# A fused agent attention and squared-ReLU layer: small products on TensorE get a timetable of chunks and one more place

## The chip, the cores and the metric

The kernel runs on one core of a Trainium2 chip. The metric is the time of one execution in microseconds of device time, as the median of several runs. A profiled execution was recorded beside them; its instructions are what the rows below show.

## What is computed

Per batch (B = 4, N = 12480 tokens of C = 128 channels, 49 agents) two softmaxes stand in a row, and their output feeds a two-layer network with squared ReLU (d_ff = 2048):

```python
def sm(a, b):
    s = scale * (a @ b.transpose(0, 2, 1))
    s = s - s.max(-1, keepdims=True)
    e = np.exp(s)
    return e / (e.sum(-1, keepdims=True) + 1e-09)
a2k = sm(agents, k)
agent_v = a2k @ v
q2a = sm(q, agents)
x = q2a @ agent_v                      # reshaped to 49920 x 128
h = np.maximum(x @ w_in, 0.0)
return h * h @ w_out
```

## The kernel before

The product `agent_v @ w_in` is folded into a table `aw` per batch (three parts: `hi` and `lo` of the agents' rows), so the first layer is a product of the softmax weights of a token (`w`, `x`) with `aw`. Tokens come in 52 blocks of 960, thirteen to a batch. A block is worked off in sixteen steps (`c` = 0..15 in the main loop, `k` over all blocks): two halves of 480 tokens, eight steps each, of which two make a pair.

**A pair on TensorE.** `first(k)` issues, for even `k`, four main first products (`h<-w,aw_hi`, 128 x 128 against 480 columns) and four row tiles (`h<-x,aw_ex`, 19 rows each, in four row groups). Then `second(k - 4)` issues twelve products into one bank `o`: four with `wo_half`, then eight with `wo_hi` and `wo_lo`. ScalarE makes `r` and `g_hi` of `h`, VectorE `gg`, a product in place of `h`, and `g_lo`; GpSimd the other `g_lo`. The order of all these on their engines is a chain, written by `queued`. The banks of `h` are three; a pair takes two, so the third `h` of a pair needs the bank that the pair before it freed with `gg`. At every eighth step `o` is done: VectorE reads it (`ob`, scaled by `down`), and `turn` flips, so that the next `o` and the small products (`psa`) exchange their two banks. The pair in which that happens has c = 4 or c = 12.

**Small products.** Beside the pairs, TensorE computes for later blocks: the scores of the queries (`queries`: eight products of 120 x 49 per block, `psa<-ag,qt`, in float32, two instructions each), four transposes of the softmax (`psa<-ident,e`), and for the next batch, in `background(b + 1)`: the scores of thirteen blocks of keys (`psa<-ag,kt`, eight products each), two products for the maxima, thirteen chunks of values (`psa<-vs,e`, eight products each), and seven products for the tables. A generator hands its products to `put`, which appends them to one list `fill`; `second` calls `share` ahead of its second, third and fourth product, so that a small product stands between two `wo_half`: places 1, 2, 3. At the first of these, `share` takes up to eight from `fill` (four where `many` is set, at c = 14 and 0) and deals them out in turn: eight as 3, 3, 2, four as 2, 1, 1; in the pair in which the bank changes, at places 2 and 3 only.

**When they come.** The generators are stepped by the main loop. `queries(g + 2)` loads `qt` at c = 2 and puts its scores at c = 14 of block g; in block g + 1 it goes on at c = 1 (`m`, `e` on VectorE), 2 (exp on ScalarE), 3 (`z`, the division on GpSimd), 8 (the transposes), 9 (`y`, `ph`, `half`), 10 (the DMAs of `w` and `x`). `background` is stepped when a credit, one per step, covers what it asked for (`yield 1`, `yield PACE`); a `yield 0` or `yield -1` asks for a spot for products: an even c, with c / 2 in `SPOTS`, or in `STILL` for the tables, and `fill` empty. While `fill` holds anything, `background` isn't stepped at all. A step may not be placed ahead of what `behind` and `marks` name; within that, each engine's order between the chain's links is the scheduler's choice.

## Time and profile before

| what | us |
|---|---|
| median of 3 runs | 1900.27 (1900.15 to 1901.13) |
| the profiled execution, its span | 1897.8 |
| outside the span, against the median | 2.5 |
| TensorE busy | 1874.5 |
| VectorE busy | 1645.2 |
| ScalarE busy | 1670.6 |
| GpSimd busy | 1334.8 |

The span is from the first to the last instruction. A line of the order of time below names the start in us from the span's start, the time from the start of the first to the end of the last of the merged instructions, the engine, the line of the code (L494 is the helper `queued`, so go by the tiles), the operation, what it writes and reads, and how many were merged; in brackets, the engine's idle time ahead of it and what ended that. The ends of matmuls are modelled and overlap the next start, so costs on TensorE are read from start to start.

### The profile page before, as it was taken

What the parts mean: (1) busy time and instruction counts of PE and PEld (TensorE: products, weight loads), DVE (VectorE), ACT (ScalarE), POOL (GpSimd) and SP (SyncE); (2) the same over time, 40 slices, a digit from 0 to 9 for tenths busy, and PEclk for the clock granted to TensorE, in tenths of its full rate; (3) what the DMA queues carried; (4) which work ended last, traced back from release to release, by engine and by line L of the source; (5) the groups of instructions that cost most, each with busy time, mean ns of one, the idle gap of its engine ahead of it and who ended that gap; (6) DMA issues with size and microseconds to landing.
All of it is one profiled execution on the core that took longest, in us unless ns stands there. A gap on an engine that the chain in (4) does not pass through costs nothing.

```text
span 1897.8 us, 31097 instructions
## 1 busy us (share of the span) xinstructions
PE 1874.5 (99%) x10848; PEld 1402.6 (74%) x10848; DVE 1645.2 (87%) x1918; ACT 1670.6 (88%) x1607; POOL 1334.8 (70%) x1270
## 2 busy tenths in 40 slices
PE   9799999999999999999999999999999999999999
PEld 9577777777678777777767877777767777777776
DVE  6877888888988888888998788888899989899887
ACT  4577999998887899999888789999888999999997
POOL 1555789896656589887666568889666676767675
PEclk9899999999999999999999999999999999999999
DMA  9233222221123222222112322222111111111110
GB/s 372 77 107 106 88 66 83 82 74 53 56 69 108 85 84 76 90 74 63 50 47 90 102 71 74 90 66 72 48 46 55 51 52 52 51 53 43 57 36 29
DMA packets 74148, 144.53 MB, mean 76 GB/s; under 512 B 9356, under 2 KB 45864, under 8 KB 73992
## 3 DMA queue, kind: packets, MB, share of 16 engines
q1 hardware_dynamic: 73992, 142.55, 23.6%
q8 instruction: 86, 1.41, 0.3%
q14 instruction: 70, 0.57, 0.1%
HBM read 82.89 MB, written 25.56 MB: 57 GB/s over the span
## 4 chain that ended last, share of the span: by engine, by line
PE 87%; DVE 7%; issue 2%; ACT 2%; POOL 1%; DMA 1%; SPq 0%; POOLq 0%; DVEq 0%; ACTq 0%
PE o L494 53%; PE h L494 24%; PE psa L494 10%; DVE gg L494 2%; ACT r L494 1%; DVE g_lo L494 1%; POOL g_lo L523 1%; ACT g_hi L494 1%; DVE h L494 1%; DMA raw<-in_w_in 1%; DVE aw_half L392 0%; DVE ob L494 0%; DMA ahead<-in_kT 0%; DVE rest L117 0%; DVE s L278 0%
## 5 line engine op out<-in xcount | busy, mean ns | idle before, releaser
L523 POOL TENSOR_TENSOR g_lo<-gg,g_hi 128x480 f16<-128x480 f32 x832 | 998.0, 1221 | 424.4 <-ACT g_hi L494 264.9
L494 ACT ACTIVATE r<-h 128x960 f32<-128x960 f32 x832 | 763.5, 967 | 113.7 <-PE h L494 56.4
L494 ACT ACTIVATE g_hi<-r 128x1920 fp32r<-128x1920 f32 x416 | 754.2, 1813 | 30.3 <-ACT r L494 0.7
L494 DVE TENSOR_TENSOR g_lo<-h,g_hi 128x960 f16<-128x960 f32 x416 | 479.9, 1154 | 126.2 <-ACT g_hi L494 93.8
L494 PE MATMUL o<-g_hi,wo_hi 128*128 128x480 f32 x1664 | 569.1, 423 | 0.0
L494 DVE TENSOR_TENSOR gg<-r,h 128x960 f32<-128x960 f32 x416 | 479.4, 1152 | 83.0 <-ACT r L494 78.7
L494 PE MATMUL o<-g_lo,wo_half 128*128 128x480 f16 x1664 | 516.9, 370 | 0.5 <-POOL g_lo L523 0.5
L494 PE MATMUL o<-g_hi,wo_lo 128*128 128x480 f32 x1664 | 496.1, 379 | 0.0
L494 DVE TENSOR_TENSOR h<-r,h 128x960 f32<-128x960 f32 x416 | 480.4, 1155 | 1.1
L494 PE MATMUL h<-w,aw_hi 128*128 128x480 f32 x1664 | 433.5, 381 | 6.9 <-DVE gg L494 4.1
L494 PEld LDWEIGHTS h<-w,aw_hi 128*128 128x128 f32 x1664 | 311.9, 189 | 62.7 <-DVE gg L494 10.7
L494 PEld LDWEIGHTS o<-g_hi,wo_hi 128*128 128x128 f32 x1664 | 314.7, 189 | 50.1 <-issue 0.8
L494 PEld LDWEIGHTS o<-g_hi,wo_lo 128*128 128x128 f32 x1664 | 312.6, 188 | 48.8
L494 PEld LDWEIGHTS <-wo_half 128*128 128x128 f16 x1664 | 171.9, 112 | 149.0 <-issue 96.7
L494 PE MATMUL h<-x,aw_ex 19*128 19x480 f16 x1664 | 159.1, 372 | 0.0
L494 PEld LDWEIGHTS <-aw_ex 19*128 19x128 f16 x1664 | 41.8, 91 | 138.3 <-issue 138.3
L494 PEld LDWEIGHTS psa<-ag,qt 128*120 128x120 f32 x816 | 127.6, 187 | 6.8 <-issue 0.3
L494 PE MATMUL psa<-ag,qt 128*120 128x49 f32 x816 | 118.3, 249 | 0.0
L428 POOL TENSOR_TENSOR e<-e,z 120x392 f32<-120x392 f32 x52 | 43.9, 845 | 74.3 <-DVE z L427 40.4
L286 POOL TENSOR_TENSOR vs<-vt,vs 120x1024 fp32r<-120x1024 f32 x39 | 85.8, 2201 | 0.0
L494 PEld LDWEIGHTS psa<-ag,kt 128*120 128x120 f32 x624 | 78.1, 184 | 5.1 <-DVE ob L494 2.5
L494 PE MATMUL psa<-ag,kt 128*120 128x49 f32 x624 | 76.7, 259 | 0.0
(147 smaller groups left out, 1086.3 us busy)
## 6 DMA issues: line engine op xcount, KB each, us to landing
qt<-in_qT SPq DMA_DIRECT2D x52, 480.0 KB
out_T<-ob SPq DMA_DIRECT2D x104, 240.0 KB
vt<-in_v SPq DMA_DIRECT2D x39, 516.0 KB
kt<-in_kT SPq DMA_DIRECT2D x39, 480.0 KB
w<-ph SPq DMA_DIRECT2D x102, 91.9 KB
w<-y SPq DMA_DIRECT2D x102, 91.9 KB
x<-half SPq DMA_DIRECT2D x416, 17.8 KB
ahead<-in_v SPq DMA_DIRECT2D x13, 516.0 KB
```

Source lines behind the costliest of these rows:

```text
L286: last[nc.gpsimd] = nc.gpsimd.tensor_sub(vs[:, :, C + 1 : 2 * C + 1], vt[:, :, :C], vs[:, :, :C].bitcast(F32))
L428: nc.gpsimd.tensor_mul(e, e, z.broadcast_to([TP, NT, NA]))
L494: ins = issue(*args, **kw)
L523: chain[nc.gpsimd] = nc.gpsimd.tensor_sub(lo[:, n, :], gg[:, n, :], hi[:, 0, n, :].bitcast(F32)).ins
```

## The change

`put` takes sizes and cuts a set of products into chunks; `fill` holds chunks, and one is taken per pair (`take`, before `first`). Its products are dealt out over places 1, 2, 3 as before, over 2 and 3 where the bank changes; a chunk of scores that goes on with a set, or has no chunk in the pair before it, uses places 1, 2, 3, 0. Place 0 is new: between the four main first products and the four row tiles, in `first`. Three plans replace the fixed numbers: "old" for blocks 0 and 1 of a batch with another to come (scores of queries put at c = 14, in 4 + 4), "dense" for blocks 2 and 3 (put at c = 12, in 3 + 5; the softmax one to two steps earlier; keys at c = 0 and 8 in 4 + 4, at c = 4 in one), "lean" for all others (put at c = 12, in 2 + 4 + 2). The sizes and the step of the put come from the plan of the next block (`then`). The maxima, values and tables ask for the same spots now ("lean": 1, 2, 3, 5), and `background` is held back only by chunks of its own, except where it wants a spot.

```diff
@@ -35,9 +35,18 @@
 PAIRED = (0, 2, 4, 6, 1, 3, 5, 7)
 OPEN = 10
 HELD = 1
-SPOTS = (1, 2, 3, 5, 6)
-STILL = (1, 3, 5)
 PACE = 1.4
+ONE = (NT,)
+TWO = (NT // 2, NT // 2)
+
+PLANS = {
+    "old": dict(put=14, sizes=TWO, early=(), late=(1, 2, 3, 8, 9, 10), spots=(1, 2, 3, 5, 6),
+                keys={p: ONE for p in (1, 2, 3, 5, 6)}),
+    "lean": dict(put=12, sizes=(2, 4, 2), early=(), late=(1, 2, 3, 8, 9, 10), spots=(1, 2, 3, 5),
+                 keys={p: ONE for p in (1, 2, 3, 5)}),
+    "dense": dict(put=12, sizes=(3, 5), early=(15,), late=(0, 1, 6, 7, 8), spots=(0, 1, 2, 4, 5),
+                  keys={0: TWO, 2: ONE, 4: TWO}),
+}
 
 
 @with_exitstack
@@ -184,13 +193,19 @@
 
 
     fill = []
-
-    def put(calls):
+    owner = [None]
+
+    def put(calls, sizes=None):
         if alone[0]:
             for call in calls:
                 call()
-        else:
-            fill.extend(calls)
+            return
+        assert not fill
+        at = 0
+        for n in sizes or (len(calls),):
+            fill.append((calls[at : at + n], sizes is not None, at > 0, owner[0]))
+            at += n
+        assert at == len(calls)
 
     def product(*args, **kw):
         def issue():
@@ -226,12 +241,12 @@
 
     def scores(b, i, kt):
         st = state.setdefault(b, {"s": []})
-        yield 0
+        sizes = yield -2
         ps = bank()
         sv = ps[:TP, : NT * NA].rearrange("p (t a) -> p t a", a=NA)
         put([
             product(sv[:, t, :], kt[:, t * TP : (t + 1) * TP], ag[:, b, :], start=True, stop=True) for t in range(NT)
-        ])
+        ], sizes)
         yield 1
         s = sp.tile([TP, NT, NA], F32, name="s")
         nc.scalar.copy(s, sv)
@@ -401,7 +416,7 @@
 
     weights = {}
 
-    def queries(g, early=None):
+    def queries(g, early=None, sizes=None):
         b = g // NB
         qt = qp.tile([C, BLK], F32, name="qt", bufs=1)
         nc.sync.dma_start(qt, qT[:, g * BLK : (g + 1) * BLK])
@@ -412,7 +427,7 @@
         put([
             product(sv[:, slots[t], :], qt[:, t * TP : (t + 1) * TP], ag[:, b, :], start=True, stop=True)
             for t in range(NT)
-        ])
+        ], sizes)
         yield
         m = qp.tile([TP, NT, 1], F32, name="m", bufs=1)
         nc.vector.reduce_max(m, sv, axis=AX.X)
@@ -507,6 +522,8 @@
             cs = slice((2 * c + n) * P, (2 * c + n + 1) * P)
             queued(nc.tensor.matmul, nc.tensor, out, state[b]["hi"][:, cs], w, start=True, stop=False)
 
+        for call in due[0]:
+            call()
         with tc.high_priority():
             for t, out in enumerate(outs):
                 rows = slice(t * 32, t * 32 + NL)
@@ -529,23 +546,32 @@
         queued(nc.vector.tensor_sub, nc.vector, lo, hs[1][:, :, :G], hi[:, 1].bitcast(F32))
         parts[k + 1] = hi[:, 1], lo
 
-    due = []
-
-    def share(n, new):
-        if n == 1:
-            calls = [fill.pop(0) for _ in range(min(len(fill), NT // 2 if many[0] else NT))]
-            due[:] = [[], [], [], []]
-            for at in range(len(calls)):
-                due[2 + at % 2 if new else 1 + at % 3].append(None)
-            for d in due:
-                for at in range(len(d)):
-                    d[at] = calls.pop(0)
-        for call in due[n]:
-            call()
+    due = [[], [], [], []]
+    busy = [False]
+
+    def take(swap):
+        for d in due:
+            d.clear()
+        before, busy[0] = busy[0], bool(fill)
+        if not fill:
+            return
+        calls, scored, on, _ = fill.pop(0)
+        if swap:
+            places = (2, 3)
+        elif scored and (on or not before):
+            places = (1, 2, 3, 0)
+        else:
+            places = (1, 2, 3)
+        counts = [len(range(n, len(calls), len(places))) for n in range(len(places))]
+        at = 0
+        for n, place in sorted(zip(counts, places), key=lambda x: x[1]):
+            due[place].extend(calls[at : at + n])
+            at += n
 
     def flush():
         while fill:
-            fill.pop(0)()
+            for call in fill.pop(0)[0]:
+                call()
 
     def second(k):
         g, i = divmod(k, SLOTS)
@@ -559,7 +585,8 @@
             todo += [(w[:, 2 * c + n, :], hi[:, n, :]) for w in (wo_hi, wo_lo) for n in range(2)]
         for n, (w, y) in enumerate(todo):
             if 0 < n < 4:
-                share(n, i % NP == 0)
+                for call in due[n]:
+                    call()
             queued(
                 nc.tensor.matmul, nc.tensor, o[:, :G], w, y,
                 start=(i % NP == 0 and n == 0), stop=(c == NP - 1 and n == len(todo) - 1),
@@ -595,12 +622,20 @@
 
     marks = []
 
-    def step(gen):
+    def waits(gen):
+        return any(of is gen for *_, of in fill)
+
+    def step(gen, sent=None):
+        assert not waits(gen)
+        owner[0] = gen
 
         with ExitStack() as es:
             for ins in behind + sum(marks[-2:-1], []):
                 es.enter_context(tc.issue_after(ins))
-            return next(gen, "end")
+            try:
+                return gen.send(sent)
+            except StopIteration:
+                return "end"
 
     def run(gen):
         for _ in gen:
@@ -679,8 +714,14 @@
 
     alone[0] = False
     ffn = ctx.enter_context(tc.tile_pool(name="ffn", bufs=4))
-    many = [False]
     later = None
+
+    def plan(g):
+        b, i = divmod(g, NB)
+        if b + 1 < B and i < 2:
+            return PLANS["old"]
+        return PLANS["dense" if i < 4 and b + 1 < B else "lean"]
+
     for k in range(total + LAG):
         if k < total:
             g, c = divmod(k, SLOTS)
@@ -694,11 +735,17 @@
             if i == 0 and c == 0 and b + 1 == B:
                 want = "end"
             credit = min(credit + 1.0, 5.0)
+            now, then = plan(g), plan(g + 1)
             for _ in range(2):
-                if want == "end" or (want <= 0 and (c % 2 or c // 2 not in (STILL if want else SPOTS))) or credit < want or fill:
+                if want == "end" or credit < want or waits(todo):
                     break
+                sent = None
+                if want <= 0:
+                    if fill or c % 2 or c >= then["put"] or c // 2 not in now["keys" if want == -2 else "spots"]:
+                        break
+                    sent = now["keys"][c // 2] if want == -2 else None
                 credit = credit - want if want > 0 else 0.0
-                want = step(todo)
+                want = step(todo, sent)
                 if k == 0:
                     credit = -6.0
                 if want is None:
@@ -707,14 +754,15 @@
             if g + 1 < B * NB:
                 if c == 0 and g:
                     ahead = later
-                if c in ((2, 3, 4, 5, 8, 9, 10) if g == 0 else (1, 2, 3, 8, 9, 10)):
+                if c in ((2, 3, 4, 5, 8, 9, 10) if g == 0 else now["late"]):
                     step(ahead)
             if g + 2 < B * NB:
                 if c == 2:
-                    later = queries(g + 2)
-                if c in (2, 14):
+                    later = queries(g + 2, sizes=then["sizes"])
+                if c in (2, then["put"], *then["early"]):
                     step(later)
-            many[0] = c in (14, 0)
+            if k % 2 == 0 and k >= LAG:
+                take((k - LAG) % NP == 0)
             if k % 2 == 0:
                 begun = first(k)
                 next(begun)
```

## Rows read from the trace of the kernel before

**Rows 1.** Page, part 1: busy us (share of the span) xinstructions

```profile
PE 1874.5 (99%) x10848; PEld 1402.6 (74%) x10848; DVE 1645.2 (87%) x1918; ACT 1670.6 (88%) x1607; POOL 1334.8 (70%) x1270
```

**Rows 2.** Waits of TensorE, whole span: us in total, times, longest

```profile
PE h L494 <- DVE gg L494: 4.1, 10, 0.8
...
PE psa L494 <- DVE ob L494: 1.6, 3, 0.7
```

**Rows 3.** Order of time, TensorE: plain pair, stalled pair, pair behind a late `gg`

```profile
1409.58 1.03 PE L494 MATMUL h<-w,aw_hi 128*128 128x480 f32 x4
...
1413.41 0.60 PE L494 MATMUL h<-w,aw_hi 128*128 128x480 f32 x2
1414.77 0.69 PE L494 MATMUL h<-w,aw_hi 128*128 128x480 f32 x2 [0.77 <-DVE gg L494]
...
1639.50 1.18 PE L494 MATMUL h<-w,aw_hi 128*128 128x480 f32 x4
```

**Rows 4.** Order of time, TensorE: quiet block, pairs at c = 14 and 0

```profile
1529.59 1.03 PE L494 MATMUL h<-w,aw_hi 128*128 128x480 f32 x4
...
1530.86 0.38 PE L494 MATMUL o<-g_lo,wo_half 128*128 128x480 f16 x1
...
1531.43 0.37 PE L494 MATMUL o<-g_lo,wo_half 128*128 128x480 f16 x1
1531.64 0.31 PE L494 MATMUL psa<-ag,qt 128*120 128x49 f32 x2
1531.79 0.37 PE L494 MATMUL o<-g_lo,wo_half 128*128 128x480 f16 x1
...
1534.07 1.03 PE L494 MATMUL h<-w,aw_hi 128*128 128x480 f32 x4
...
1538.56 1.03 PE L494 MATMUL h<-w,aw_hi 128*128 128x480 f32 x4
```

**Rows 5.** Order of time, TensorE: two pairs with keys, c = 2 and 4

```profile
121.29 1.03 PE L494 MATMUL h<-w,aw_hi 128*128 128x480 f32 x4
...
126.62 1.03 PE L494 MATMUL h<-w,aw_hi 128*128 128x480 f32 x4
...
132.13 0.38 PE L494 MATMUL h<-w,aw_hi 128*128 128x480 f32 x1
```

**Rows 6.** Order of time, weight loads of TensorE: the first pair of rows 4

```profile
1530.55 0.10 PEld L494 LDWEIGHTS <-aw_ex 19*128 19x128 f16 x4 [0.33 <-issue]
...
1530.86 0.61 PEld L494 LDWEIGHTS psa<-ag,qt 128*120 128x120 f32 x4
```

**Rows 7.** Groups by line: busy us, mean ns of one, idle before

```profile
L494 PE MATMUL psa<-ag,qt 128*120 128x49 f32 x816 | 118.3, 249 | 0.0
L494 PE MATMUL psa<-ag,kt 128*120 128x49 f32 x624 | 76.7, 259 | 0.0
L392 DVE CAST aw_half<-aw_lo 49x512 f16<-49x512 f32 x16 | 14.3, 894 | 0.4 <-DMA aw_ex<-aw_half 0.2
L387 DVE SCALAR_TENSOR_TENSOR aw_lo<-psa,rl,aw_hi 49x512 fp32r<-49x512 f32 x12 | 8.7, 725 | 0.0
```

**Rows 8.** Order of time, VectorE: quiet block from c = 0; late `gg`

```profile
1536.60 1.16 DVE L494 TENSOR_TENSOR gg<-r,h 128x960 f32<-128x960 f32 x1 [0.66 <-ACT r L494]
1537.67 0.56 DVE L418 TENSOR_REDUCE m<-psa 120x8 f32<-120x392 f32 x1
...
1545.27 1.15 DVE L494 TENSOR_TENSOR gg<-r,h 128x960 f32<-128x960 f32 x1
...
1558.92 0.71 DVE L494 TENSOR_SCALAR ob<-o,down 128x480 f32<-128x480 f32 x1
...
1638.76 1.15 DVE L494 TENSOR_TENSOR gg<-r,h 128x960 f32<-128x960 f32 x1 [0.35 <-issue]
```

**Rows 9.** Order of time, VectorE: an eviction of the tables beside `gg`

```profile
462.95 0.15 DVE L359 TENSOR_TENSOR bound<-psa,rl 98x1 f32<-98x1 f32 x1
463.17 1.15 DVE L494 TENSOR_TENSOR gg<-r,h 128x960 f32<-128x960 f32 x1
```

## The prediction

> **What bounds the kernel now.** I read the page's engine line first, then TensorE's waits, then its order of time pair by pair. A pair is the work of one even step: four main first products (`h<-w`), four row tiles (`h<-x`), four `wo_half` products with the small products among them, eight further `o` products; sixteen steps c = 0..15 make a block. TensorE is busy for 1874.5 us, 99% of the span [rows 1], and it waits longest in total for VectorE's `gg`, 4.1 us [rows 2]. So the time is the sum of what TensorE is given, and the reader should look at what a pair costs with and without small products. A pair without any takes 1413.41 - 1409.58 = 3.83 us [rows 3]. One with four score products of a row set takes 4.48, at c = 14 and again at c = 0 (1529.59, 1534.07, 1538.56) [rows 4]: 0.66 more. One with eight of keys takes 5.33, and 5.51 where they stand at two places only [rows 5].
>
> **Two prices.** At c = 14 the four stand 2, 1, 1 behind the first three `wo_half`; in the first key pair the eight stand 3, 3, 2. With s for the first product at a place and a for each further one, 3s + a = 0.66 and 3s + 5a = 1.50, so a = 0.21 and s = 0.15. The order of time says the same: two products between two `wo_half` make 1530.86 to 1531.43 = 0.57 us, one makes 0.36 (1531.43 to 1531.79) [rows 4], none 0.21. A product alone has its first weight load behind the 480 columns before it; one behind another product does not. Each product that leaves a neighbour and gets a place of its own saves 0.06 us.
>
> On this the Trainium skill (TensorE: Matmul & The Clock Gate, Part 3, The mechanism) speaks against the change: a weight load overlaps with running products only where the row groups differ. A score product fills the same rows as the `wo_half` before it, so by that rule nothing would be hidden, place or no place, and s would equal a. The two prices above do not agree with it; the load row shows the loads of `psa` starting at 1530.86, with the `wo_half` product [rows 6].
>
> **Row sets.** 816 instructions, two to a product, are 51 sets of eight [rows 7]; the first is issued in one go before the pairs begin to overlap, and the planner places 50. Its credits and spots, followed step by step through the code, give for the old version the pairs that the trace shows, and for the new one the counts below. Now a set costs 2 x 0.66 = 1.32. Under "lean" (39 of the 50) it becomes 2 + 4 + 2 products at c = 12, 14, 0, all alone, seven behind `wo_half` and one at place 0: 7 x 0.15 + p, with p the price of place 0. Under "old" (5 sets) seven of ten groups become 1, 1, 1, 1 and three stay 2, 1, 1. Under "dense" (6 sets) the groups are 2, 1 and 1, 2, 1, 1: five alone, two behind another, one at place 0: as dear as now.
>
> **Place 0** does not occur in the old trace, so p has to be bounded. Now the loads of the row tiles start at 1530.55, 0.33 us after the weight loads before them ended [rows 6], and 0.96 after the first of four `h` (1529.59) [rows 4]; with 0.22 from one `h` to the next that is 0.30 after the fourth, some 0.09 more than its columns need. A product in between has its first load behind the fourth `h`, as behind a `wo_half`; its second load shows, and the row tiles then wait their 0.09 as they did. So p = 0.15 to 0.16, nearest to the row of a product alone; I take 0.16. Below: if the 0.09 covered part of the second load, 0.10 or somewhat less. Above: 0.25, if the pause came twice. Place 0 is used 61 times (52 of rows, 9 of keys).
>
> So a lean set costs 1.05 + 0.16 = 1.21, 0.12 less than now within rounding: 39 x 0.12 = 4.6 us. The seven "old" groups save 0.05 each: 0.4. Dense: 0.
>
> **Keys.** 39 chunks of eight [rows 7]. Now 24 stand 3, 3, 2 (1.50 each) and 15 at two places (1.65, between 1.59 and the 1.68 of rows 5): 60.8 us. Then 17 stand 3, 3, 2, 13 at two places, and 9 are cut into 2, 1, 1 (0.66) and 1, 1, 1, 1 (0.61): 25.5 + 21.5 + 11.4 = 58.4. Saved: 2.3.
>
> **Background moved.** The maxima of the keys cost a stall where a product sits in the pair that changes banks and waits for `ob` (1.6 us in three [rows 2]); in the first batch it leaves that pair: about 0.6 saved. Later in each batch the four products that make `aw` now stand at least four steps apart; with the new spots three of them fall on c = 2, 4, 6 of one block. Each brings VectorE 0.73 + 0.89 = 1.62 us [rows 7], and a plain pair leaves it about 0.4 (3.83 less three operations of 1.15 [rows 8]). The old spacing already costs a stall of 0.77 before an `h` [rows 3], about 2 us in all such places of a batch. Closer together, but in longer pairs, I put them at 2.5: 3 x 0.5 = 1.5 lost, between 0 and 3. Values keep their pairs but for one or two chunks per batch. The steps that a waiting fill used to hold back may now go at c = 15 and 0; they are of other engines, the fullest of which, ScalarE, is busy for 88% of the span [rows 1]: nothing. The DMA of `qt` stays at c = 2, those of `w` and `x` at c = 10 (c = 8 in six dense blocks), with SyncE's queue otherwise as it was: nothing.
>
> **What the earlier products wait for.** In the pair at c = 12 they use the bank that `ob` has just read. `ob` ends at 1558.92 + 0.71 = 1559.63 in a quiet block [rows 8], 1.52 after that pair's start; the first product there comes at 1.69, with its load 0.2 earlier. That is barely free; in blocks with values `ob` is earlier.
>
> **What is late next.** The pair at c = 0 shrinks from 4.48 to 4.13. Just behind it VectorE is full: `m`, `e`, `z` of the softmax, then `gg` of c = 4, which ends at 1545.27 + 1.15 = 1546.42, 12.35 after c = 0 began [rows 8]. The third `h` of the pair at c = 6 needs that buffer. It would now stand at 4.13 + 2 x 3.83 + 0.44 = 12.22, so it would wait 0.2 us, and the next load with it. What decides is where `m` goes. Now the last score product stands behind the third `wo_half` and ends 1.27 + 0.57 + 0.36 + 0.21 + 0.31 = 2.72 after the pair's start [rows 4], at 1536.8, after `gg` started (1536.60), and VectorE has idled 0.66 us before that `gg`; `m` comes behind it, at 1537.67 [rows 8]. In the new order the last one stands behind the second `wo_half` and ends 1.27 + 0.36 + 0.21 + 0.31 = 2.15 after the start, 1536.2 in these rows. `m` (0.56) then fits largely into the idle time, and the chain ends some 0.3 earlier. That a small eviction is put ahead of `gg` when its product ends early has an example: `bound` at 462.95, before `gg` at 463.17 [rows 9]. I count on it: nothing lost.
>
> **The sum.** -4.6 - 0.4 - 2.3 - 0.6 + 1.5 = -6.4 us. The profiled execution spans 1897.8 us and the median is 1900.27; the 2.5 around the span does not depend on the change. 1897.8 - 6.4 = 1891.4, or 1893.9 as a median: I forecast 1894.0. That is 0.33% faster; 0.2% (3.8 us) is about what can be told from no change.
>
> **Rivals.**
> (1) VectorE takes the gain back. If `m` stays behind `gg`, each quiet lean block (11 of them, where TensorE has no values) waits 0.19 and loses the cover of one load. A late `gg`, ending at 1639.91, 0.41 after its pair began [rows 3, 8], made four `h` take 1.18 in place of 1.03 [rows 3, 4]. That is 0.19 + 0.10 = 0.29, times 11. In the 18 lean blocks with values, which are longer, I count one lost cover each, 0.12, as a bound. Together 5.4 lost: 1899.4. For it: VectorE without a gap through these pairs. Against it: rows 9.
> (2) Place 0 is cheaper, 0.10: 61 x 0.06 = 3.7 more gained, 1890.3. For it: the 0.09 pause is there anyway. Against: no row shows a weight load in it.
> (3) Place 0 is dearer, 0.25: 61 x 0.09 = 5.5 lost, 1899.5.
> (4) Slower: the four loads of the row tiles, which now start together within 0.10 us [rows 6], come one after another behind a small product, 3 x 0.09 later: p = 0.43, 61 x 0.27 = 16.5 lost, 1910.4. It turns slower from p = 0.27 on. Against it: those loads already wait until the `h` before them is through.
> (5) Places do not matter. If a lone product cost what a neighbour does, only the terms of the background would stay: 1900.27 - 0.6 + 1.5 = 1901.2. The page's rule above would give this; the two prices speak against it.
>
> **How the numbers follow.** Forecast 0.57, (1) 0.20, (2) 0.09, (3) 0.06, (4) 0.05, (5) 0.03. The forecast's own range is 1891 to 1897 (tables 0 to 3, the rest from rounding); 0.06 of its 0.57 lies above 1896.5. Range: down to (2) with nothing lost on the tables, 1889.5; up to (1) or (3), 1899.6. Left out: (4), (5) and edges, under 0.2. Faster by over 0.2%: 0.51 + 0.09 = 0.60. Slower by over 0.2%: (4) and a bad case of (1) with (3), 0.07. Within: 0.33.
>
> **What the new profile would show.** Pairs at c = 12, 14, 0 of a quiet block at 4.13, 4.43, 4.13 us (now 3.83, 4.48, 4.48). From the fourth `h` over a product at place 0 to the row tiles 0.46 where it is 0.30 now: this gives p. `m` ahead of `gg` in the pair at c = 0, and no wait of `h` for `gg` at c = 4 and 6; if `m` stands behind, (1). The tables' blocks at 11 and 12 of a batch longer by about half a us in sum. The forecast is wrong if p is above 0.25, if the stalls for `gg` come once per block, or if VectorE's backlog under three `aw` products in a row grows past 3 us in all.

## The result and the profile after

| | median, us | profiled span, us |
|---|---|---|
| before | 1900.27 (1899.67 to 1901.13, 5 runs) | 1897.8 |
| after | 1910.78 (1910.06 to 1911.09, 5 runs) | 1909.3 |

The ratio is 1.0054, 95% interval 1.0042 to 1.0067. The changed kernel is about half a per cent slower, where I had forecast 0.33% faster with a range that ended at 1899.6.

The engine line of the page, to be held against [rows 1], says little: TensorE is as full as it was, for 6.2 us longer, and the other engines do the same work.

```profile
PE 1880.7 (99%) x10848; PEld 1412.7 (74%) x10848; DVE 1647.1 (86%) x1918; ACT 1670.2 (87%) x1607; POOL 1335.0 (70%) x1270
```

TensorE's waits after (us in total, times, longest), to be held against [rows 2]. The waits for `gg` sum to no more than before, though one of them is now 1.4 long. New are a wait for a DMA, 1.7 us, and waits of the tables' own products for a bank that VectorE's `aw_lo` reads, 1.2 us.

```profile
PE h L509 <- DVE gg L509: 3.8, 4, 1.4
...
PE psa L509 <- DMA kt<-in_kT: 1.7, 1, 1.7
PE psa L509 <- DVE aw_lo L402: 1.2, 3, 0.4
```

Since waits and busy time do not tell where 11.5 us of span come from, I measured every block from the start of its first `h` to that of the next block's, in both traces, and summed the differences over blocks that do the same kind of work (us against the kernel before, one profiled execution each; the three last columns belong to experiments told further down; 1.6 of the +4.9 under "gate" is a drop of the clock that other executions do not have in that block):

| blocks | number | after | gate | gate_no_max | before_no_max |
|---|---|---|---|---|---|
| block 0 | 1 | +7.0 | +1.6 | +1.5 | +0.2 |
| "old" | 5 | -2.8 | -1.7 | -3.2 | -0.6 |
| "dense" | 6 | -3.9 | -2.7 | -2.7 | -0.7 |
| fifth block of batches 0 to 2 | 3 | +2.7 | +4.9 | -0.6 | -0.6 |
| lean, with values | 13 | +1.7 | +1.7 | -1.4 | -0.2 |
| lean, quiet | 11 | +1.7 | +1.9 | -1.5 | -0.3 |
| lean, with tables | 11 | +4.1 | +4.1 | -1.6 | -2.8 |
| start, last two blocks | | +1.0 | 0.0 | -0.2 | +0.4 |
| sum | | +11.5 | +9.8 | -9.8 | -4.6 |

There are four places that lose: block 0, the fifth blocks, the tables, and a little in each of the 24 other lean blocks. Each can be read from the trace.

**The quiet block.** Order of time on TensorE, pairs at c = 14, 0, 2, 4 and 6 (columns as in [rows 4]):

```profile
1539.54 1.03 PE L509 MATMUL h<-w,aw_hi 128*128 128x480 f32 x4
1540.41 0.31 PE L509 MATMUL psa<-ag,qt 128*120 128x49 f32 x2
1540.65 0.38 PE L509 MATMUL h<-x,aw_ex 19*128 19x480 f16 x4
...
1543.96 1.03 PE L509 MATMUL h<-w,aw_hi 128*128 128x480 f32 x4
...
1548.12 1.04 PE L509 MATMUL h<-w,aw_hi 128*128 128x480 f32 x4
...
1551.95 1.15 PE L509 MATMUL h<-w,aw_hi 128*128 128x480 f32 x4
...
1555.90 1.16 PE L509 MATMUL h<-w,aw_hi 128*128 128x480 f32 x4
...
1559.86 0.38 PE L509 MATMUL h<-w,aw_hi 128*128 128x480 f32 x1
```

The pairs with products take 4.42 (c = 14) and 4.16 (c = 0), as forecast. But the plain pairs at c = 4 and 6 take 3.95 and 3.96 in place of 3.83, and their four `h` span 1.15 and 1.16 in place of 1.03. The weight loads of the pair at c = 4, and VectorE from c = 0 on, say why:

```profile
1551.74 0.40 PEld L509 LDWEIGHTS h<-w,aw_hi 128*128 128x128 f32 x2
1552.39 0.30 PEld L509 LDWEIGHTS h<-w,aw_hi 128*128 128x128 f32 x2 [0.25 <-DVE gg L509]
```

```profile
1546.49 1.15 DVE L509 TENSOR_TENSOR gg<-r,h 128x960 f32<-128x960 f32 x1 [0.45 <-ACT r L509]
1547.56 0.56 DVE L433 TENSOR_REDUCE m<-psa 120x8 f32<-120x392 f32 x1
...
1551.19 1.16 DVE L509 TENSOR_TENSOR gg<-r,h 128x960 f32<-128x960 f32 x1
...
1555.16 1.15 DVE L509 TENSOR_TENSOR gg<-r,h 128x960 f32<-128x960 f32 x1
```

`m` stands behind `gg` as before, VectorE idles 0.45 us ahead of that `gg`, and the chain behind it is as long as it was: the third `gg` ends 1555.16 + 1.15 - 1543.96 = 12.35 after the pair at c = 0 began, to the hundredth what [rows 8] gave. The `gg` of c = 2 ends at 1552.35, and the third weight load of the next pair goes at 1552.39. TensorE comes earlier by what the pair at c = 0 lost, and stands. The matmul rows show no idle time there; the load row does. Over the whole span the group of these loads (busy us, mean ns, idle ahead of it and its main releaser) has 13.6 us behind `gg`, the kernel before 10.7; in the eleven quiet blocks alone it is 5.9 against 1.2:

```profile
L509 PEld LDWEIGHTS h<-w,aw_hi 128*128 128x128 f32 x1664 | 310.8, 189 | 65.4 <-DVE gg L509 13.6
```

VectorE has no idle time between that first `gg` and the third. But the `gg` of c = 2 (1551.19) also starts only 0.10 after the first of the two `r` in the row below is done (1551.09), and that `r` stands behind an exponential for which ScalarE waited 0.54 us, until VectorE had made `e` (ScalarE):

```profile
1549.69 0.53 ACT L437 ACTIVATE e<-e 120x392 f32<-120x392 f32 x1 [0.54 <-DVE e L435]
1550.13 1.82 ACT L509 ACTIVATE r<-h 128x960 f32<-128x960 f32 x2
```

So `m` and `e` behind the scores delay that `gg` in two ways, in VectorE's own order and by way of ScalarE.

**Blocks with values** lose in the pair at c = 2. The first product with values waits for the bank that VectorE's `e` reads until 775.92 + 0.56 = 776.48 (order of time, VectorE and TensorE):

```profile
775.92 0.56 DVE L435 TENSOR_TENSOR e<-psa,m 120x392 f32<-120x392 f32 x1
```

```profile
776.21 0.38 PE L509 MATMUL o<-g_lo,wo_half 128*128 128x480 f16 x1
776.62 0.57 PE L509 MATMUL psa<-vs,e 120*98 120x258 f32 x3
```

0.41 us lie between these two starts; in the kernel before it is 0.17 (770.88 and 771.05). The pair takes 5.11, before 4.87.

**Block 0.** Windows of the profile (busy us and number of instructions of PE, PEld, DVE, ACT, POOL; granted clock; DMA share; GB/s), first before, then after:

```profile
86.00:90.00 4.00, 4.00 (x16) 2.16 (x16) 2.96 (x5) 1.70 (x3) 2.36 (x2) 0.57 0.32 66
90.00:94.00 4.00, 4.00 (x28) 3.15 (x26) 3.50 (x6) 3.94 (x4) 1.65 (x2) 1.00 1.00 382
```

```profile
86.00:90.00 4.00, 4.00 (x17) 2.65 (x17) 3.50 (x5) 1.83 (x2) 2.12 (x3) 0.50 0.17 32
90.00:94.00 4.00, 2.32 (x11) 1.70 (x10) 3.19 (x6) 3.80 (x4) 1.15 (x2) 0.50 0.97 359
94.00:99.40 5.40, 5.40 (x20) 4.73 (x20) 1.63 (x2) 0.74 (x2) 2.36 (x2) 0.51 0.81 285
```

TensorE has fallen to its lower level (1.2 GHz, 0.50) after the pauses of the first pairs in both kernels. Before, it is back at 2.4 GHz from some 89 on; now it stays at 0.50 up to 99.3, though in the stretch from 94 on it is busy throughout. Beside it the first products with keys, which came at c = 6, now stand at c = 4 and wait for their DMA:

```profile
92.33 1.81 PE L509 MATMUL psa<-ag,kt 128*120 128x49 f32 x8 [1.68 <-DMA kt<-in_kT]
...
94.33 1.68 PE L509 MATMUL psa<-ag,kt 128*120 128x49 f32 x8
```

Eight instructions in 1.68 us are some 0.20 each, at half the clock. The pair takes 12.09 us where it took 5.41. They moved because `scores` now asks with -2 where it asked with 0: the credit starts at -6 and rises by one per step, and `credit < want` lets -2 pass at step 4.

**The fifth block of a batch.** In the second batch's (block 17) the values come at c = 4, in the pair that changes banks; before they came at c = 2. Order of time on TensorE, ScalarE, VectorE and GpSimd:

```profile
708.31 0.60 PE L509 MATMUL h<-w,aw_hi 128*128 128x480 f32 x2
710.28 0.70 PE L509 MATMUL h<-w,aw_hi 128*128 128x480 f32 x2 [1.37 <-DVE gg L509]
```

```profile
705.81 0.51 ACT L307 ACTIVATE d<-d 120x392 f32<-120x392 f32 x1
706.35 0.52 ACT L284 CAST e<-d 120x392 fp32r<-120x392 f32 x1
706.77 0.53 ACT L437 ACTIVATE e<-e 120x392 f32<-120x392 f32 x1
707.21 1.81 ACT L509 ACTIVATE r<-h 128x960 f32<-128x960 f32 x2
```

```profile
707.97 1.21 DVE L441 TENSOR_SCALAR z<-z 120x8 f32<-120x8 f32 x1
709.09 1.14 DVE L509 TENSOR_TENSOR gg<-r,h 128x960 f32<-128x960 f32 x1
```

```profile
706.73 2.41 POOL L540 TENSOR_TENSOR g_lo<-gg,g_hi 128x480 f16<-128x480 f32 x2
```

Two delays add up. Three operations of the softmaxes stand in a row on ScalarE ahead of `r`. And `gg` needs only the first of the two `r` in that row, which is done at 708.16; it starts at 709.09, since VectorE is busy until then with the small `z` of the softmax. This operation takes 0.16 or 0.17 us in 49 of the 52 blocks, with no operation of GpSimd running beside it. In the other three, blocks 4, 17 and 30, it starts while a `g_lo` runs on GpSimd, takes 0.52, 1.21 and 1.19 us, and ends 0.03 us after that `g_lo` (here 709.17 against 709.14). In this block 0.93 of the 1.37 us that TensorE waits lie behind `z`. The pair takes 6.96.

**The tables.** The loss sits in the pairs that hold their products: in blocks 24 and 25 five of these take 4.24, 4.28, 4.94, 4.89 and 5.37 us, where a run told below (gate_no_max) has 3.94, 3.99, 4.69, 4.69 and 4.91 in the same places. The loads of `h` wait less for `gg` in the blocks with tables than before, 1.4 against 7.5 us; here it is the tables' products that wait, for a bank that VectorE has yet to read.

### The profile page after: what moved, and what is told of

Its sections match the earlier page's. It is cut to its first block, busy times and chain, and to the rows that moved or that the text cites. A ratio compares the mean times of both kernels' runs of the same rounds, so it can differ in the third digit from the quotient of the medians.

```text
span 1909.3 us, 31122 instructions
## 1 busy us (share of the span) xinstructions
PE 1880.7 (99%) x10848; PEld 1412.7 (74%) x10848; DVE 1647.1 (86%) x1918; ACT 1670.2 (87%) x1607; POOL 1335.0 (70%) x1270
## 4 chain that ended last, share of the span: by engine, by line
PE 88%; DVE 6%; ACT 3%; issue 2%; DMA 1%; POOL 0%; SPq 0%; POOLq 0%; DVEq 0%; ACTq 0%
PE o L509 53%; PE h L509 24%; PE psa L509 10%; ACT r L509 1%; DVE gg L509 1%; ACT g_hi L509 1%; PE h L213 1%; DVE h L509 1%; DVE ob L509 1%; DVE g_lo L509 0%; PE h L658 0%; DVE rest L126 0%; DVE s L293 0%; DMA out_T<-ob 0%; DVE rest L127 0%
## 5 line engine op out<-in xcount | busy, mean ns | idle before, releaser
L509 PE MATMUL o<-g_lo,wo_half 128*128 128x480 f16 x1664 | 525.0, 370 | 1.0 <-POOL g_lo L540 0.5
L509 PEld LDWEIGHTS h<-w,aw_hi 128*128 128x128 f32 x1664 | 310.8, 189 | 65.4 <-DVE gg L509 13.6
L509 PEld LDWEIGHTS psa<-ag,qt 128*120 128x120 f32 x816 | 139.6, 187 | 18.7 <-DVE ob L509 6.2
L509 PE MATMUL psa<-ag,qt 128*120 128x49 f32 x816 | 127.2, 243 | 0.4 <-DVE ob L509 0.2
L509 PEld LDWEIGHTS psa<-ag,kt 128*120 128x120 f32 x624 | 85.2, 188 | 8.2 <-issue 2.5
L509 PE MATMUL psa<-ag,kt 128*120 128x49 f32 x624 | 81.8, 259 | 1.7 <-DMA kt<-in_kT 1.7
```

The costliest lines, as they stand in the source:

```text
L509: ins = issue(*args, **kw)
```

## The experiments

Two theories stood against each other at first. One: the loss sits in block 0, by the DMA and the clock, and a repair of that leaves most of the forecast gain. The other: VectorE decides in all lean blocks (rival 1), and the gain on TensorE is given back there.

**early_keys.** The first tile of keys of batch 1 is loaded ahead of the pairs; they stay at c = 4.

```diff
-        kt = load_keys(b, 0, kv, "kt")
+        kt = first_keys.pop() if first_keys else load_keys(b, 0, kv, "kt")
...
                     raws = [load_w_out(n) for n in range(NW)]
+                    first_keys.append(load_keys(1, 0, kv, "kt"))
```

> The changed kernel (1910.8 us), with the tile of the first keys of batch 1 loaded before the pairs begin, and its timetable untouched. In the changed kernel's trace the first chunk of keys stands one pair earlier (block 0, c = 4), waits 1.68 us for the DMA of kt, and TensorE stays at half its clock until 99.3 us (89.4 before); block 0 is 7.0 us longer. Theory A (the wait for the DMA keeps the clock down and costs nearly all of block 0's loss): block 0 about 40 us, 1904. Rival A2 (the clock stays down for another reason, the wait alone counts): 1909. Rival A3 (block 0 is a disturbance of the profiled run alone): 1910.8 as before.

Measured: 1908.77 us (1904.74 to 1910.18), ratio 1.0038 (1.0025 to 1.0051). The wait for the DMA is gone, the products are not cheaper (order of time, TensorE):

```profile
90.04 1.69 PE L509 MATMUL psa<-ag,kt 128*120 128x49 f32 x8
...
91.93 1.68 PE L509 MATMUL psa<-ag,kt 128*120 128x49 f32 x8
```

Block 0 still loses 4.3 us, and the low clock lasts 13.7 us in this trace. The runs themselves fall into two groups, two at 1904.7 and 1905.0, which is theory A's number, and three from 1908.8 to 1910.2, which is A2's. The two experiments below that are built on this one (put14, sizes341) have the same instructions in the same order in these pairs of block 0, and block 0 loses 2.2 and 6.0 us, with 10.2 and 20.5 us at the low clock. So the rest of block 0's loss goes with the time at the low clock, in which the products with keys take twice as long, and that time differs between executions of the same instructions; what the DMA's wait alone costs, one trace of each does not tell.

**before_key4.** The kernel before, with nothing but its first products with keys let in at c = 4.

```diff
-                    credit = -6.0
+                    credit = -4.0
```

> The kernel before (1900.3 us) with one number changed, the credit that the background starts with (-4 for -6), so that its first chunk of keys comes at c = 4 of block 0 as in the changed kernel; one chunk less comes in block 2. Theory A: the wait for the DMA and the half clock appear here too, 1900.3 + 6.7 = 1907. Rival A2 (they belong to the new timetable): 1900.

Measured: 1905.19 us (1903.54 to 1905.71), ratio 1.0024 (1.0014 to 1.0033). Block 0 loses 6.7 us, 1.5 come back because a later block has one chunk of keys less. The low clock lasts 20.5 us, and the wait for the DMA is there:

```profile
91.70 1.81 PE L494 MATMUL psa<-ag,kt 128*120 128x49 f32 x8 [1.12 <-DMA kt<-in_kT]
```

So moving the first chunk of keys by one pair, without any other part of the change, makes the loss of block 0; its span and the low clock are one execution's, but all ten runs are slower than every one of the kernel before.

**gate.** The changed kernel with the first keys back at c = 6. The first batch then needs a third block by the "old" plan for all its work to fit.

```diff
-        if b + 1 < B and i < 2:
+        if b + 1 < B and i < (2 if b else 3):
...
-                if want == "end" or credit < want or waits(todo):
+                if want == "end" or credit < max(want, 0) or waits(todo):
```

> The changed kernel (1910.8 us), but a spot for products also needs a credit of zero or more, so the first chunk of keys comes at c = 6 of block 0 as in the kernel before, behind the stretch at half clock; so that the timetable still closes, batch 0 runs three blocks under the plan old (two in the changed kernel). The first keys loaded early gave 1904.7 to 1910.2 by the length of the stretch at half clock. Theory A' (the early key products themselves, at half clock, and the longer stretch are the loss, not only the DMA): block 0 back to 39.2 us, all runs close together, 1910.8 - 7.6 = 1903.5. Rival (the stretch stays long without them): block 0 above 42, 1907.

Measured: 1909.36 us (1908.64 to 1909.86), ratio 1.0047 (1.0032 to 1.0062). The expected 1903.5 is missed. Block 0 is repaired (+1.6 in place of +7.0, though the low clock lasts 13.7 us here too), and the time hardly moves: block 4 of the first batch, which had lost 0.3 us only, now also gets its values at c = 4, and that pair goes from 4.81 to 8.53 us (with a drop of the clock to 0.50 behind its wait, worth some 1.6 us against the same pair of blocks 17 and 30), and "old" and "dense" together gain 4.4 in place of 6.7. The first theory is thus true for block 0 and false for the rest: with block 0 out of the way there is no gain.

**put14.** early_keys, with the lean sets put at c = 14 in 4 + 4, as before, but dealt over places 1, 2, 3, 0. The pair at c = 12 stays plain.

```diff
-    "lean": dict(put=12, sizes=(2, 4, 2), ...
+    "lean": dict(put=14, sizes=TWO, ...
```

> As early_keys, but under the plan lean the scores of the queries are put at c = 14 in 4 + 4 and not at c = 12 in 2 + 4 + 2, so that the pair at c = 0 is 4.43 us long again and two products of a set stand at place 0. Theory B (the loss of the lean blocks is that the pair at c = 0 got shorter while VectorE's work behind it did not: 0.25 us of waits at c = 4 and 6 in a quiet block, 0.24 at c = 2 in a block with values): 12 x 0.25 + 17 x 0.24 = 7 us less than early_keys, about 1897, quiet blocks near 32.24 us. Rival C (place 0 is dear, 0.43 a product): 39 x 0.28 = 11 us more than early_keys.

Measured: 1901.92 us (1898.9 to 1904.47), ratio 1.0007 (0.9998 to 1.0017). Against early_keys that is the 7 us of theory B, but not in its places: the traces have 3.3 of them in the quiet blocks and those with values, where it said 7, the others in block 0, the "dense" and the fifth blocks. In the quiet blocks c = 14 and c = 0 are shorter than in the kernel before by 0.06 and 0.05, and c = 6 is longer by 0.12: the sum is nil (32.41 us, expected 32.24). Even 0.05 us less at c = 0 comes back behind VectorE. Rival C is out. The blocks with values are at par with the kernel before, where the change loses 0.13 in each.

**sizes341.** early_keys, with the lean sets in 3 + 4 + 1 in place of 2 + 4 + 2, so that one product only is left for c = 0.

```diff
-    "lean": dict(put=12, sizes=(2, 4, 2), ...
+    "lean": dict(put=12, sizes=(3, 4, 1), ...
```

> As early_keys, but the sets of the plan lean are cut 3 + 4 + 1 at c = 12, 14, 0: one product of a set gets a neighbour (0.06 us, 39 sets, 2.4 us more on TensorE), and the last one stands at the first place of c = 0. In the built program m of the softmax then stands ahead of gg on VectorE, where it stood behind gg in 2 + 4 + 2. Theory B (VectorE's order behind c = 0): the waits at c = 2 to 6 go, 7 us, so 1904 + 2.4 - 7 = 1899. Rival (the waits come from the shorter pair whatever the order): 1906.

Measured: 1902.88 us (1901.16 to 1906.83), ratio 1.0016 (1.0007 to 1.0025). Here the scores end early enough, and the scheduler does what I had counted on (VectorE):

```profile
1539.75 0.56 DVE L433 TENSOR_REDUCE m<-psa 120x8 f32<-120x392 f32 x1
1540.28 1.16 DVE L509 TENSOR_TENSOR gg<-r,h 128x960 f32<-128x960 f32 x1
...
1548.61 1.15 DVE L509 TENSOR_TENSOR gg<-r,h 128x960 f32<-128x960 f32 x1
```

The third `gg` now ends 1548.61 + 1.15 - 1537.75 = 12.01 after c = 0 began, 0.34 earlier than before, as the prediction had reckoned ("some 0.3"). But with one product the pair at c = 0 is 0.5 shorter, and TensorE still stalls, in this block at c = 6 alone (pairs at c = 4, 6 and 8):

```profile
1545.56 1.04 PE L509 MATMUL h<-w,aw_hi 128*128 128x480 f32 x4
1549.39 1.13 PE L509 MATMUL h<-w,aw_hi 128*128 128x480 f32 x4
1553.33 1.03 PE L509 MATMUL h<-w,aw_hi 128*128 128x480 f32 x4
```

Against early_keys the blocks with values gain 2.8, the tables 3.3, the quiet ones 1.1 us: `m` ahead of `gg` is worth what I had assumed in kind, but the quiet blocks still are no shorter than before (32.46 us against 32.40). The median lies midway between theory B's 1899 and the rival's 1906.

**gate_no_place0.** gate without place 0.

```diff
-        elif scored and (on or not before):
-            places = (1, 2, 3, 0)
```

> As gate, but no chunk uses place 0: what stood there gets a neighbour at places 1 to 3. Theory (a product at place 0 costs 0.15 us, as read from the changed kernel's trace, and one with a neighbour 0.21; place 0 lies in pairs that TensorE bounds): 61 x 0.06 = 3.5 us more than gate, 1907. Rival C (place 0 is what made the change slow): less than gate, 1900 or below. Rival (waits swallow it): 1903.5 as gate.

Measured: 1910.62 us (1909.29 to 1911.28), ratio 1.0053 (1.0038 to 1.0068). The sign is that of the prices, the size is not: 1.3 us at the medians where the prices alone give 3.5. The quiet blocks lose 0.08 each, those with values 0.06. Place 0 is not what made the kernel slower.

**gate_341_spots.** gate with 3 + 4 + 1 and with the background's spots in lean blocks at c = 2, 6, 10 only.

```diff
-    "lean": dict(put=12, sizes=(2, 4, 2), ..., spots=(1, 2, 3, 5),
+    "lean": dict(put=12, sizes=(3, 4, 1), ..., spots=(1, 3, 5),
```

> As gate, with the sets of lean cut 3 + 4 + 1 (m ahead of gg on VectorE) and lean's spots for the background at c = 2, 6, 10 (no values or tables in the pair that changes banks, tables at least four steps apart). Theory B with the tables as the second cost: sizes341 left the 13 blocks with values 1.0 us under the kernel before in sum, the quiet ones 0.6 over and the tables' blocks 0.8 over; with the values moved from c = 4 the three blocks at 4 of a batch lose their 3.7: about 1896, below the kernel before. Rival (the losses in the blocks at 4 and the tables come from the earlier start of the background, wherever it stands): 1900.

Measured: 1899.56 us (1898.22 to 1900.8), ratio 0.9993 (0.9984 to 1.0003): the same as before, and the rival's number, not theory B's. The tables go from +4.1 (gate) to +0.2, the values from +1.7 to -1.0. The fifth blocks keep +2.8. Their values now come at c = 6, and the pair at c = 4, with no small product in it, still takes 5.28 us in block 17, since it still waits for `gg`:

```profile
706.25 0.70 PE L509 MATMUL h<-w,aw_hi 128*128 128x480 f32 x2 [1.18 <-DVE gg L509]
```

So it is not the place of the values that costs. ScalarE has the same three operations ahead of `r` there (from 701.77 to 703.01), but the first `r` is done at 703.98 and `gg` starts at 705.05: between them VectorE works through `g_lo` and two operations of `z`, the second again a long one (0.63 us).

**gate_no_max and before_no_max.** If VectorE holds TensorE back, the gain must appear when VectorE has less to do behind c = 0. In both kernels the softmax of the queries was left without its maximum.

```diff
-        m = qp.tile([TP, NT, 1], F32, name="m", bufs=1)
-        nc.vector.reduce_max(m, sv, axis=AX.X)
         e = qp.tile([TP, NT, NA], F32, name="e", bufs=1)
-        nc.vector.tensor_sub(e, sv, m.broadcast_to([TP, NT, NA]))
-        yield
-        nc.scalar.activation(e, e, AF.Exp, scale=scale)
+        if early:
...
+        yield
+        nc.scalar.activation(e, e if early else sv, AF.Exp, scale=scale)
```

Only the first block of all (`early`) keeps the maximum; the other 51 leave it out.

> As gate, but the softmax of the queries behind the first block leaves out the maximum and its subtraction: ScalarE takes the exponential from the bank itself, and VectorE is spared m and e, 2 x 0.56 us behind c = 0 of each block. Theory B (VectorE's work behind the shorter pair at c = 0 makes the waits at c = 2 to 6): 0.25 in 11 quiet blocks and 0.24 in 17 with values go, and a little in others: 7 us less than gate, 1896.5; quiet blocks 32.25 us. Rival (the waits come from ScalarE or from the banks): as gate.

> The kernel before with the softmax of the queries without its maximum and subtraction on VectorE (ScalarE's exp reads the bank of the scores; the maximum is left out, only the first two blocks keep it), the same edit as in gate_no_max. Theory A, the places are worth what I summed and VectorE was in the way: the kernel before hardly stalls in its quiet blocks, so it gains little by the edit (its waits for gg, some 3.8 us, and the tables' stalls of about 2), 1895 to 1897, and gate_no_max (1889.7) stays 5 to 7 us below it; quiet blocks here 32.3 to 32.4 us, c = 14 and c = 0 at 4.48, c = 12 at 3.83. Theory B, the places give nothing and dropping VectorE's work is all: 1889 to 1891, the same as gate_no_max. Theory C, the before kernel does not profit at all: 1900.

Measured: gate_no_max 1889.73 us (1888.34 to 1889.96), ratio 0.9942 (0.9928 to 0.9957); before_no_max 1895.29 us (1894.12 to 1896.68), ratio 0.9975 (0.9964 to 0.9986). The same edit is worth 19.6 us to gate and 4.5 to the kernel before (1899.77 in the same round), and 5.6 us lie between the two in favour of the timetable, as theory A had it. The 19.6 are far more than the 7 expected of gate_no_max: 6.4 come from the quiet blocks and those with values, 5.6 from the tables, 5.6 from the fifth blocks (1.6 of it the clock that dropped in gate's trace). In the trace of gate_no_max (from c = 0 of a quiet block) the pair with products takes 4.15 and the plain ones 3.83 each, c = 4 and 6 too:

```profile
1526.05 1.03 PE L510 MATMUL h<-w,aw_hi 128*128 128x480 f32 x4
1530.20 1.04 PE L510 MATMUL h<-w,aw_hi 128*128 128x480 f32 x4
1534.03 1.03 PE L510 MATMUL h<-w,aw_hi 128*128 128x480 f32 x4
1537.86 1.03 PE L510 MATMUL h<-w,aw_hi 128*128 128x480 f32 x4
1541.69 1.03 PE L510 MATMUL h<-w,aw_hi 128*128 128x480 f32 x4
```

In before_no_max the same stretch is that of the kernel before, 4.48 and 3.83:

```profile
1529.78 1.03 PE L495 MATMUL h<-w,aw_hi 128*128 128x480 f32 x4
1534.26 1.03 PE L495 MATMUL h<-w,aw_hi 128*128 128x480 f32 x4
1538.09 1.03 PE L495 MATMUL h<-w,aw_hi 128*128 128x480 f32 x4
```

The loads of `h` wait 3.1 us for `gg` in gate_no_max and 6.4 in before_no_max, against 14.3 in gate. This tells the theories apart: the timetable is worth about what was summed, and the two operations behind the scores keep it from the end. The edit does not tell by which way: it takes `m` and `e` off VectorE, and with them the exponential's wait for `e` on ScalarE, and the bank of the scores is read by ScalarE. That VectorE's order counts by itself is what sizes341 shows, where `m` stays and changes its place, together with gate_341_no_max below. gate_no_max is faster than both kernels; whether exponentials without a maximum are safe depends on the size of the scores, and no run here puts that to the test.

**gate_341_no_max.** gate_no_max with 3 + 4 + 1. It asks whether 3 + 4 + 1 was better in itself or by VectorE's order alone.

> gate_no_max with the lean sets in 3, 4, 1 in place of 2, 4, 2 (at c = 12, 14, 0). With the maximum left out, VectorE's place behind the scores no longer matters. If the gain of 3, 4, 1 in sizes341 (3 us in the blocks of values and tables) was all VectorE's order, it is gone here: per set three more or less alone products are the same by the prices (7 at 0.15, one at place 0), so 1889.7 within 1. If it was something of the pair at c = 0 itself (its length against ScalarE or the weight loads), 1886.5 to 1887.5.

Measured: 1889.51 us (1889.38 to 1891.31), ratio 0.9943 (0.9926 to 0.9959), no different from gate_no_max, as expected if the gain of 3 + 4 + 1 was all VectorE's order. Measured in the same round as before_no_max, it also confirms the distance between the timetables: 5.8 us.

## Why the prediction was wrong

**Right: the two prices and place 0.** The pairs at c = 14 and 0 came out at 4.42 and 4.16, forecast 4.43 and 4.13. Place 0 costs, from the fourth `h` over the product to the row tiles, 0.458 us against 0.306 without it, as medians over the trace's 61 and 355 places: p = 0.152, forecast 0.16. The four loads of the row tiles still start together:

```profile
1540.20 0.39 PEld L509 LDWEIGHTS psa<-ag,qt 128*120 128x120 f32 x2
1540.65 0.10 PEld L509 LDWEIGHTS <-aw_ex 19*128 19x128 f16 x4
```

Rivals 2, 3 and 4 fall with that. The time measured, 1910.8, is almost the 1910.4 of rival 4, but by coincidence: its p of 0.43 is not there. Rival 5 falls with the pair at c = 14, shorter by the price of one neighbour (4.42 for 4.48), and with gate_no_max against before_no_max: equal prices would have left little between them, and 5.6 us are there. The rule of the Trainium skill (TensorE: Matmul & The Clock Gate, Part 3, The mechanism) that a weight load overlaps only where row groups differ is not what this trace shows: the load of the product at place 0 starts at 1540.20, 0.21 ahead of its matmul (1540.41), while an `h` with the same rows is running. The same section also lets a load into the background weight buffer be pulled ahead, which would fit; the trace does not name the buffer.

**Near, with `m` and `e` gone: the sum, in part by luck.** Between before_no_max and gate_no_max the lean sets gain 0.105 (quiet blocks) and 0.09 (values) each, forecast 0.12. Block 0 apart, 6.5 us are gained in the traces, forecast 6.4. But the terms do not agree so well, and gate is not quite the changed kernel: "old" and "dense" gain 4.7, forecast 3.3 with rows, keys and maxima; start and end gain 0.6, forecast nothing; and the blocks with tables lose 1.2, although some ten lean sets in them should have given back most of the 1.5 forecast.

**Wrong: "What is late next".** This step ended with "nothing lost", and it failed twice. It counted on `m` moving ahead of `gg` because the last score product ends earlier; it did not move. `bound` in [rows 9] was an example of something ready in time, not of a product that ends in the idle time ahead of `gg`; in sizes341, with the scores ended still earlier, `m` does go first. And the deadline was set at the third `h`'s matmul; it is that matmul's weight load, which row 1552.39 shows waiting 0.25 where the matmuls lose 0.12. With the load as deadline, 0.22 earlier, both c = 4 and c = 6 are late: at c = 4 it is 4.16 + 3.83 + 0.44 - 0.22 = 8.21 against a `gg` that ends at 8.39. That is rival 1, to which I gave 0.20. Its price per quiet block, 0.29, was about right: the two plain pairs are 0.24 longer, and the block ends 0.155 longer than before where it should have been 0.12 shorter. In the blocks with values the loss has another place, the bank that `e` reads: they end 0.13 longer.

**Wrong: "Keys".** I counted where the 39 chunks stand and took the movement of the first one by two steps for free. It cost 7.0 us in the profiled execution, the largest single term: 1.7 of waiting for a DMA that had been hidden, about 1.5 for the chunk itself, which a later block no longer has, and the rest from products that run at half the clock and from a clock that stays low longer. That rest differs between executions of the same instructions (early_keys). The row that would have warned is the granted clock of the stretch: 0.57 at 86 to 90 in the trace of before. I had read the clock for the whole span only.

**Wrong in size: "Background moved".** The blocks with tables lose 4.1 where the bound was 3 and the term 1.5, and they hold some ten lean sets that were to gain 1.2, so the term measures about 5.3. In sizes341 they lose 0.8 and in gate_no_max, against before_no_max, 1.2, so most of the excess is VectorE's backlog again. The step had the wait wrong, too: it priced stalls of an `h` behind `gg`, and what waits is the tables' products, for their bank. For the values I had written that they keep their pairs "but for one or two chunks per batch". Those chunks stand in the fifth block: 2.7 us in three blocks, where two softmaxes' exponentials and a cast meet ahead of `r` and a `z` beside GpSimd's `g_lo` takes up to 1.21 us ahead of `gg`. The work of the other engines that goes on earlier I had costed at nothing, by ScalarE's mean load of 88% [rows 1]. The wait stays in gate_341_spots, where no small product is in the pair. It all but goes in gate_no_max, where the exponential finds an earlier slot, ScalarE's other two operations stand one ahead of each `r`, and a whole `g_lo` lies between the long `z` and `gg`: the pair falls from 6.92 to 5.59 us. No run moved these operations alone, so how much each of them costs stays open.

**The account.** 7.0 (block 0) + 2.7 (fifth blocks) + 4.1 (tables) + 3.4 (other lean blocks) + 1.0 (start and end) - 6.7 ("old" and "dense", of which 1.5 is the chunk of keys that block 0 took over, if before_key4 carries over) = 11.5 us. The 1.0 is not explained; the start alone, where next to nothing was changed, varies from -1.0 to +0.6 between the traces.

## What to carry to other kernels

Where TensorE is full, a shorter pair can be worth nothing until the engine that hands buffers back is earlier too, as in the lean blocks here: set the deadline at the weight load, not at the matmul, and follow the chain over the next three pairs, through every engine in it. Taking two operations of 0.56 us per block off the second engine turned gate's loss into about the gain that had been summed. And when a planner's condition is loosened, step it through the very first block: what is moved there meets data that has not landed and a clock that is not yet up.

## What the hardware showed

- A stall of TensorE behind a late buffer can be invisible in its matmul rows: the load row shows 0.25 us of waiting, the four `h` take 1.15 in place of 1.03, and the matmuls' list of waits has 3.8 us for `gg`, where the loads have 13.6.
- The stretch at the lower clock in block 0 lasted 6.8 us before, 17.1 after, 20.5 in before_key4 and 13.7 in gate. With the same instructions in these pairs it lasted 13.7 us in early_keys, 10.2 in put14 and 20.5 in sizes341, and block 0 lost 4.3, 2.2 and 6.0 us: one profile of such a stretch is one draw. At 0.50 a pass of a small product took 0.20 us, and TensorE was busy for 5.40 of 5.40 us of such a stretch: a full engine in the profile is not an engine at its clock.
- A small product at a place of its own cost 0.15 us behind the main first products as it does between two `wo_half`, though the row tiles behind it change to another shape.
- A small operation of VectorE (`z`, 120x8) took 0.16 or 0.17 us in 49 places where GpSimd was idle, and 0.52, 1.21 and 1.19 us in the three where a `g_lo` was running on GpSimd; each time it ended 0.03 us after that `g_lo`. The traces of before, gate, sizes341 and gate_no_max say the same: every long `z` (2, 3, 3 and 5 of 52) started beside an operation of GpSimd and ended 0.03 us after it, and no short one did. Its row shows it as busy, so no list of waits has it.
